# Moving a group's small work from before the scores to behind them, in a fused attention and soft mixture-of-experts kernel

## The chip, the cores and the metric

One Trainium2 chip, of which the kernel uses one core. The metric is device time in microseconds (us) of one execution, lower is better. TensorE is called PE here, its weight loads PEld, VectorE DVE, ScalarE ACT, GpSimd POOL and SyncE SP.

## The reference

```python
scale = 1.0 / S                                  # S = 2496, 8 batches, D = 256, d_qk = 64
attn = np.maximum(scale * (z @ z.T), 0.0) ** 2   # per batch
x = u * (attn @ v)                               # all tokens together: N = 19968
logits = x @ phi                                 # 32 slots: 8 experts of 4
d = softmax of logits over the tokens            # each slot's weights
slot_input = d.T @ x
slot_out = per expert: relu(slot_input @ w1) @ w2
c = softmax of logits over the slots             # each token's weights
out = c @ slot_out
```

The kernel computes all of it in one launch, with the transposed output.

## The kernel before

**Tiling.** The attention runs per batch over chunks of up to 512 queries (`chunks`, L150; a batch is 4 x 512 + 448, and the last one ends in two chunks of 256), and per chunk over 5 steps p of four key tiles of 128. A step has two half steps s = 0 and 1. `pair(i, w)` (L454) makes the scores of two key tiles of step i: six PE matmuls into the two tiles sc (L180 to L195), on ACT two relus and two squares (r, L199 and L203), on DVE the high part ph and the low part pl of each square (L205, L211). `attend` (L215) has the weighted sums of step i in its two half steps, 24 matmuls each into acc, from ph, pl and v; half step s first calls `between(s)`, which calls `pair(i + 1, s)`. So the scores run one step ahead of the sums that use them: the first half of a step needs the ph and pl that the half step before has made.

**The group's small work.** When 1024 tokens are done, `finish_chunk` (L275) starts a generator `groups(q)` (L292) and puts six calls of it into `work`; `between` takes one a half step, from p = 1 on. Call 1: the logits of the group into the PSUM tile lg (32 PE instructions in the trace), and into the same tile the slot sums of the group before it (`late`, `slot_sums`, L389; 32 more); on DVE the block that makes L, the running maximum and m (L316 to L324). Call 2 does nothing. Calls 3 and 4: sixteen transpositions each of the group's x into the tiles tr_0 and tr_1 (L335), and ACT's copy xt of each. Call 5: eight transpositions of L and E into the tile le and ACT's copy of it. There are 20 groups; 19 start inside the attention.

**What sets the order.** PE, ACT and DVE run in program order (`InOrder`, L39); each engine's queue is the order in which the code issues. Three lists hold closures for later: `begin` is emptied at the head of `between`, `middle` inside `scores` between the relus and the squares (L201), `behind` at the end of `scores` (L213). Into `middle` goes `exps` (the exponential E on ACT, L326), into `behind` goes `add_up` (L400: three DVE instructions that add the slot sums to slot_acc, reading the tile lg) and the splits of the next batch's z and v that have landed (`landing`). The tiles lg, tr, le and sl share the tag "ms" of `ms_ps` (L61), which has one buffer of two banks: a new one starts when the last reader of the one before is done.

Of the kernel before, what the change touches and what calls it, by code (L numbers as in the profile page):

```python
# [50 lines left out]
def attn_soft_moe_kernel(ctx, tc, uT, v, zz, phi, ww, outT):  # L51
# [19 lines left out]
    def load_z(b, j):  # L71
        raw = raws.tile([P, 512], F32, tag="zraw" if b == 0 else "raw", name=f"zr_{b}_{j}", bufs=NQ if b == 0 else NRAW)
        nc.sync.dma_start(raw, zz[b, :, j * 512 : (j + 1) * 512])
        zraw[b, j] = raw

        def split():
            t = zt[b, j] = blk.tile([P, 2, 512], F32R, tag="blk", name=f"z_{b}_{j}")
            for h in (1, 0):
                rows = HALF[h]
                act.copy(t[rows, h], raw[rows])  # L80
                dve.tensor_sub(t[rows, 1 - h], raw[rows], f32(t[rows, h]))

        return split

    def load_v(b, i):
        raw = raws.tile([P, 2, D], F32, tag="raw", name=f"vr_{b}_{i}", bufs=NRAW)
        nc.sync.dma_start(raw, v[b, :, 2 * i : 2 * i + 2, :])

        def split():
            t = vt_[b, i] = blk.tile([P, 2, 2, D], F32R, tag="blk", name=f"v_{b}_{i}")  # L90
            act.copy(t[:, :, 0], raw)
            dve.tensor_sub(t[:, :, 1], raw, f32(t[:, :, 0]))

        return split
# [8 lines left out]
    def open_loads(m):  # L103

        while opening and (len(v_splits) < m or opening[0][0] is load_z):
            f, j = opening.pop(0)
            (z_splits if f is load_z else v_splits).append(f(0, j))
# [61 lines left out]
    def run(todo):  # L169
        now, todo[:] = todo[:], []  # L170
        for f in now:
            f()

    def scores(b, ch, p, w):


        j, o, n, t0 = ch
        k0 = 4 * p + 2 * w
        ps = [sc_ps.tile([P, QC], F32, tag="sc", name=f"sc_{t0}_{k0 + h}") for h in range(2)]
        if t0 == 0:  # L180
            for h, rows in enumerate(HALF):
                c = 2 * w + h
                pe.matmul(
                    ps[h], zraw[b, p][rows, c * P : (c + 1) * P], zraw[b, 0][rows],
                    start=True, stop=True,
                )
        else:
            zk, zq = zt[b, p], zt[b, j]
            for m, (kl, ql) in enumerate(((0, 0), (0, 1), (1, 0))):
                for h, rows in enumerate(HALF):  # L190
                    c = 2 * w + h
                    pe.matmul(
                        ps[h][:, :n], zk[rows, h ^ kl, c * P : (c + 1) * P],
                        zq[rows, h ^ ql, o : o + n], start=(m == 0), stop=(m == 2),
                    )  # L195
        rs = []
        for h in range(2):
            r = wa.tile([P, QC], F32, tag="r", name=f"r_{t0}_{k0 + h}", bufs=5)
            act.activation(r[:, :n], ps[h][:, :n], AF.Relu, scale=1.0 / S)  # L199
            rs.append(r)  # L200
        run(middle)  # L201
        for kt, r in enumerate(rs, k0):
            act.activation(r[:, :n], r[:, :n], AF.Square)  # L203
            hi = wa.tile([P, QC], F32R, tag="ph", name=f"ph_{t0}_{kt}", bufs=7)
            dve.tensor_copy(hi[:, :n], r[:, :n])  # L205
            if t0 == N - 256 and kt == KT - 1:
                lo, rows = hi, HALF[1]
            else:
                lo = wa.tile([P, QC], F32R, tag="pl", name=f"pl_{t0}_{kt}", bufs=7)
                rows = HALF[1] if kt == KT - 1 else slice(0, P)  # L210
            dve.tensor_sub(lo[rows, :n], r[rows, :n], f32(hi[rows, :n]))  # L211
            pend[t0, kt] = hi, lo
        run(behind)  # L213

    def attend(b, ch, p, acc, between):  # L215


        j, o, n, t0 = ch
        todo = [[[], []], [[], []]]
        for kt in range(4 * p, 4 * p + 4):  # L220
            hi, lo = pend.pop((t0, kt))
            vt = vt_[b, kt // 2][:, kt % 2]
            hh, lh, hl = (vt[:, 0], hi), (vt[:, 1], hi), (vt[:, 0], lo)
            if kt < KT - 1:
                for s in range(2):
                    for h in range(2):
                        todo[s][h] += [hh, lh, hl]
            else:

                todo[0][0] += [hh, lh]  # L230
                todo[0][1] += [lh, hl]
                todo[1][0] += [hh]
                todo[1][1] += [hl]
        for s in range(2):
            between(s)
            before = turns[-1:]
            for i in range(len(todo[s][0])):
                for h, rows in enumerate(HALF):
                    vp, pp = todo[s][h][i]
                    c = h ^ s  # L240
                    x = pe.matmul(
                        acc[:, c, :n], vp[rows, c * P : (c + 1) * P], pp[rows, :n],
                        start=(p == 0 and s == 0 and i == 0),
                        stop=(p == NP - 1 and s == 1 and i == len(todo[s][h]) - 1),
                    )
                    while before:
                        await_(x, before.pop())
            turns.append(nc.gpsimd.nop())
            await_(turns[-1], x)
# [8 lines left out]
    def attend_whole(b, ch, p, acc):  # L258

        j, o, n, t0 = ch  # L260
        for kt in range(4 * p, 4 * p + 4):
            hi, lo = pend.pop((t0, kt))
            vt = vt_[b, kt // 2][:, kt % 2]
            prods = [(vt[:, 0], hi), (vt[:, 1], hi)] + ([] if lo is hi else [(vt[:, 0], lo)])
            for c in range(2):
                for i, (vp, pp) in enumerate(prods):
                    pe.matmul(
                        acc[:, c, :n], vp[:, c * P : (c + 1) * P], pp[:, :n],
                        start=False, stop=(kt == KT - 1 and i == len(prods) - 1),
                    )  # L270
# [161 lines left out]
    def load_w(pool, tag):  # L432
        i = len(w_raw)
        if i < NW:
            t = pool.tile([P, 2, 512], F32, tag=tag, name=f"w_{i}")
            nc.sync.dma_start(t, ww[i].rearrange("p (k n) -> p k n", k=2))
            w_raw.append(t)
# [4 lines left out]
    def load_u(b, ch):  # L442
        _, _, n, t0 = ch
        ut = wa.tile([P, 2, QC], F32, tag="ut", name=f"ut_{t0}", bufs=1)
        q0 = t0 - b * S
        nc.sync.dma_start(
            ut[:, :, :n], uT[b, :, q0 : q0 + n].rearrange("(c p) q -> p c q", p=P)
        )
        ut_[t0] = ut
# [4 lines left out]
    def pair(i, w):  # L454

        if i >= len(steps):
            run(middle)
            run(behind)
            return
        b, ch, p = steps[i]  # L460
        j, t0, q = ch[0], ch[3], 2 * p + w
        if q == 2:
            load_u(b, ch)
        if len(landing) > 1:
            behind.append(landing.pop(0))
        if b < B - 1:
            if j == NQ - 3 and w:
                landing.append(load_z(b + 1, p))
            m = -1
            if j == NQ - 2 and w:  # L470
                m = p
            elif j == NQ - 1 and q in (2, 4, 5, 7, 8):
                m = NQ + (2, 4, 5, 7, 8).index(q)
            if m >= 0:
                landing.append(load_v(b + 1, m))
        elif t0 >= N - 512 - 256 and t0 < N - 256:
            if len(w_raw) < NBLK - 15:
                load_w(blk, "blk")
        elif t0 == N - 256 and q >= 2:
            load_w(blk, "blk")  # L480
        if i % (NQ * NP) == 0 and w == 0 and landing:
            behind.append(landing.pop(0))
        scores(b, ch, p, w)
        if i < NP:
            v_splits.pop(0)()
            open_loads(NRAW)
        if b == 0 and z_splits and q % 2 and t0 + q >= 5:
            z_splits.pop(0)()
# [6 lines left out]
    for i, (b, ch, p) in enumerate(steps):  # L495
        if p == 0:
            acc = acc_ps.tile([P, 2, QC], F32, tag="acc", name=f"acc_{ch[3]}")

        def between(s):
            run(begin)  # L500
            if work and 2 * p + s > 1:
                work.pop(0)()
            pair(i + 1, s)

        if i + 1 < len(steps):
            attend(b, ch, p, acc, between)
        else:
            attend_whole(b, ch, p, acc)
        if p == NP - 1:
            finish_chunk(b, ch, acc)  # L510
# [223 lines left out]
```

## Time and profile before

| | before |
|---|---|
| median of 3 runs | 1521.64 us (1521.44 to 1525.31) |
| the profiled execution | 1521.83 us |
| its span, first to last instruction | 1519.6 us |
| mean granted PE clock | 0.987 |
| ACT's wait for scores | 367.5 us in 308 waits |
| DVE's wait for ACT's squares | 263.6 us in 261 waits |

All times in the prediction's rows come from the profiled execution and count from its first instruction; the time of the run is 2.2 us more than the span. A row of the timeline gives start, length, engine, line, operation, what is written and from what, the shapes, and in brackets the idle time in front and what ended it. Most of the lines read L47, since `InOrder` issues for all; so one goes by the tiles' names, in which buffer numbers are left out. "x6" merges six like instructions.

### The profile page before, as it was taken

The page shows a single profiled execution, that of the slowest core. Times are in us where ns is not written, and L with a number is a line of the kernel's source. Part 1 is how long each engine was busy: PE and PEld are TensorE (multiplying, and loading weights), DVE is VectorE, ACT ScalarE, POOL GpSimd, SP SyncE. Part 2 cuts the span into 40 slices and gives each one's busy share as a digit, 9 for nine tenths or more (in the row PEclk, how much of TensorE's full clock was granted, in tenths as well). Part 3 has the DMA queues.
Part 4 walks back from the last instruction along what each step waited for, and adds up shares of the span by engine and source line. Part 5 has one row for each costly group of instructions (what it writes and reads, how often), then busy time and mean ns, then how long its engine had stood idle before and what let it go on. Part 6 is the DMA issues. An engine that isn't in the chain of part 4 may idle for free.

```text
span 1519.6 us, 36942 instructions
## 1 busy us (share of the span) xinstructions
PE 1484.9 (98%) x14724; PEld 1226.0 (81%) x14724; DVE 1112.4 (73%) x2205; ACT 1025.7 (67%) x1987; POOL 3.2 (0%) x21
## 2 busy tenths in 40 slices
PE   8999999999999999999999999999999999999985
PEld 7987988788787888779777888789878798888853
DVE  6778776877678776787778776787767787676753
ACT  7777756867677766777567766677667776665543
POOL 0000000000000000000000000000000000000000
PEclk9999999999999999999999999999999999999995
DMA  4111100121001210111101120011101131000759
GB/s 133 29 36 49 56 23 27 42 56 50 16 22 50 55 36 15 36 50 55 26 19 56 42 57 16 22 50 55 36 15 36 50 118 54 16 15 9 264 226 392
DMA packets 36652, 91.53 MB, mean 60 GB/s; under 512 B 3712, under 2 KB 6272, under 8 KB 34432
## 3 DMA queue, kind: packets, MB, share of 16 engines
q1 hardware_dynamic: 36480, 89.18, 18.3%
q8 instruction: 116, 1.90, 0.5%
q14 instruction: 56, 0.46, 0.1%
HBM read 68.71 MB, written 20.45 MB: 59 GB/s over the span
## 4 chain that ended last, share of the span: by engine, by line
PE 91%; DVE 4%; DMA 2%; issue 1%; ACT 1%; DVEq 0%; SPq 0%; ACTq 0%
PE acc L47 67%; PE sc L47 18%; PE lg L47 2%; DMA outT<-ot 2%; PE tr L47 1%; DVE ph L47 1%; DVE pl L47 1%; DVE z L47 1%; PE h L582 0%; PE po L604 0%; DVE ot L664 0%; PE le L47 0%; PE pf L658 0%; ACT r L47 0%; DVE slot_acc L47 0%
## 5 line engine op out<-in xcount | busy, mean ns | idle before, releaser
L47 PE MATMUL acc<-ph,v 64*128 64x512 f32 (+2 forms) x6384 | 1009.8, 384 | 0.1
L47 PEld LDWEIGHTS acc<-ph,v 64*128 64x128 f32 x6384 | 638.9, 185 | 109.2 <-DVE ph L47 3.8
L47 ACT ACTIVATE r<-sc 128x512 f32<-128x512 f32 (+2 forms) x820 | 428.5, 575 | 369.8 <-PE sc L47 367.5
L47 PE MATMUL acc<-pl,v 64*128 64x512 f32 (+2 forms) x3190 | 666.2, 384 | 1.4
L47 DVE TENSOR_TENSOR pl<-r,ph 128x512 fp32r<-128x512 f32 (+4 forms) x819 | 546.0, 667 | 74.2 <-DVE ph L47 0.9
L47 DVE CAST ph<-r 128x512 fp32r<-128x512 f32 (+2 forms) x820 | 335.7, 409 | 266.6 <-ACT r L47 263.6
L47 ACT ACTIVATE r<-r 128x512 f32<-128x512 f32 (+2 forms) x820 | 455.2, 611 | 0.0
L47 PEld LDWEIGHTS acc<-pl,v 64*128 64x128 f32 x3190 | 336.4, 184 | 63.0 <-DVE pl L47 11.2
L47 PE MATMUL sc<-z,z 64*128 64x512 f32 (+2 forms) x1920 | 276.4, 385 | 0.0
L47 PEld LDWEIGHTS sc<-z,z 64*128 64x128 f32 x1920 | 181.8, 185 | 35.8 <-issue 6.6
L47 PE MATMUL sc<-z 64*128 64x512 f32 (+2 forms) x480 | 69.4, 386 | 0.0
L47 ACT COPY xt<-tr 128x1024 f32<-128x1024 f32 x39 | 39.6, 1015 | 28.8 <-PE tr L47 28.8
L47 DVE TENSOR_TENSOR z<-zr,z 64x512 fp32r<-64x512 f32 x80 | 55.0, 687 | 2.5
L47 DVE TENSOR_TENSOR v<-vr,v 128x512 fp32r<-128x512 f32 x80 | 54.9, 686 | 1.1 <-ACT v L47 0.8
L47 ACT CAST v<-vr 128x512 fp32r<-128x512 f32 x80 | 49.4, 618 | 8.9 <-PE sc L47 8.9
L47 PEld LDWEIGHTS sc<-z 64*128 64x128 f32 x480 | 45.6, 185 | 7.7 <-issue 1.6
L47 ACT CAST z<-zr 64x512 fp32r<-64x512 f32 x80 | 49.6, 620 | 2.0
L47 DVE TENSOR_TENSOR xg<-acc,ut 128x1024 f32<-128x1024 f32 (+7 forms) x56 | 48.8, 893 | 1.8 <-PE acc L47 1.8
L664 DVE COPY ot<-pf 128x1024 f32<-128x1024 f32 (+2 forms) x22 | 24.2, 1101 | 21.3 <-DMA outT<-ot 15.5
L658 PE MATMUL pf<-cp,soh 32*128 32x512 f32 (+2 forms) x176 | 24.5, 539 | 13.6 <-ACT ot L664 9.1
L664 ACT COPY ot<-pf 128x1024 f32<-128x1024 f32 (+2 forms) x22 | 20.2, 917 | 25.2 <-DMA outT<-ot 18.3
L658 PEld LDWEIGHTS pf<-cp,soh 32*128 32x128 f32 x176 | 12.9, 239 | 24.6 <-ACT ot L664 17.0
(92 smaller groups left out, 400.2 us busy)
## 6 DMA issues: line engine op xcount, KB each, us to landing
vr<-in_v SPq DMA_DIRECT2D x80, 256.0 KB, 2.7
w<-in_w SPq DMA_DIRECT2D x32, 512.0 KB, 6.6
outT<-ot SPq DMA_DIRECT2D x16, 1024.0 KB, 8.4
ut<-in_uT SPq DMA_DIRECT2D x31, 512.0 KB, 3.7
zr<-in_zz SPq DMA_DIRECT2D x40, 256.0 KB, 2.7
ut<-in_uT SPq DMA_DIRECT2D x8, 448.0 KB, 3.5
outT<-ot SPq DMA_DIRECT2D x4, 512.0 KB, 5.1
outT<-ot SPq DMA_DIRECT2D x2, 768.0 KB, 5.6
```

The costliest lines, as they stand in the source:

```text
L47: return lambda *a, **k: self.tc.keep_in_program_order(f(*a, **k))
L658: nc.tensor.matmul(pf[t // 2][:, t % 2, :ng], a[rows, c], parts[g0][rows, k, :ng], start=(m == 0), stop=(m == 2), tile_position=(t * NS, 0),)
L664: x = (nc.vector.tensor_copy if tp else nc.scalar.copy)(o, pf[tp][:, :, :ng])
```

## The change

In `between`, the group's piece of work is taken after `pair` instead of before it:

```diff
         def between(s):
             run(begin)
+            pair(i + 1, s)
             if work and 2 * p + s > 1:
                 work.pop(0)()
-            pair(i + 1, s)
```

No instruction is added or taken away. On PE, here for group 4 (the names hold the chunk's first token, 5504, the key tile 12 or 13, and the group), before:

```order
L47 MATMUL acc_5504_5916<-pl_5504_7_5986,v_2_3_4776 128x512 x2
L47 MATMUL tr_4_0_6154<-ident_76,xg_4_4846 128x64 x16
L47 MATMUL sc_5504_12_6172<-z_2_1_4040,z_2_3_4279 128x512
L47 MATMUL sc_5504_13_6173<-z_2_1_4040,z_2_3_4279 128x512
...
L47 MATMUL acc_5504_5916<-ph_5504_8_6070,v_2_4_4922 128x512 x4
```

and now:

```order
L47 MATMUL acc_5504_5916<-pl_5504_7_5986,v_2_3_4776 128x512 x2
L47 MATMUL sc_5504_12_6154<-z_2_1_4022,z_2_3_4279 128x512
L47 MATMUL sc_5504_13_6155<-z_2_1_4022,z_2_3_4279 128x512
...
L47 MATMUL tr_4_0_6176<-ident_76,xg_4_4846 128x64 x16
L47 MATMUL acc_5504_5916<-ph_5504_8_6026,v_2_4_4922 128x512 x4
```

The transpositions of call 3 have gone from in front of the six scores to between them and the sums; lg, tr_1 and le do the same in their half steps.

On DVE, from the last instruction of the block that makes m (call 1) to the first ph behind slot_acc, before:

```order
L47 TENSOR_SCALAR m_4_6048<-runmax0_84 128x1
L47 CAST ph_5504_8_6070<-r_5504_8_6063 128x512
L47 TENSOR_TENSOR pl_5504_8_6072<-r_5504_8_6063,ph_5504_8_6070 128x512
L47 CAST ph_5504_9_6075<-r_5504_9_6065 128x512
L47 TENSOR_TENSOR pl_5504_9_6077<-r_5504_9_6065,ph_5504_9_6075 128x512
L47 SCALAR_TENSOR_TENSOR slot_acc1_83<-slot_acc0_82,m_3_4985,lg_4_6013 128x256
L47 SCALAR_TENSOR_TENSOR slot_acc1_83<-slot_acc0_82,m_3_4985 128x1
L47 TENSOR_TENSOR slot_acc1_83<-slot_acc1_83,lg_4_6013 128x256
L47 CAST ph_5504_10_6120<-r_5504_10_6115 128x512
```

and now:

```order
L47 TENSOR_SCALAR m_4_6070<-runmax0_84 128x1
L47 CAST ph_5504_10_6117<-r_5504_10_6110 128x512
L47 TENSOR_TENSOR pl_5504_10_6119<-r_5504_10_6110,ph_5504_10_6117 128x512
L47 CAST ph_5504_11_6122<-r_5504_11_6112 128x512
L47 TENSOR_TENSOR pl_5504_11_6124<-r_5504_11_6112,ph_5504_11_6122 128x512
L47 SCALAR_TENSOR_TENSOR slot_acc1_83<-slot_acc0_82,m_3_5009,lg_4_6035 128x256
L47 SCALAR_TENSOR_TENSOR slot_acc1_83<-slot_acc0_82,m_3_5009 128x1
L47 TENSOR_TENSOR slot_acc1_83<-slot_acc1_83,lg_4_6035 128x256
L47 CAST ph_5504_12_6167<-r_5504_12_6162 128x512
```

The block and slot_acc both stand one pair later: behind the pair of tiles 8 and 9, and behind that of 10 and 11.

On ACT, around the exponential E, before:

```order
L47 ACTIVATE r_5504_8_6063<-sc_5504_8_6055 128x512
L47 ACTIVATE r_5504_9_6065<-sc_5504_9_6056 128x512
L47 ACTIVATE E_4_6047,m_4_6048<-L_4_6046,m_4_6048 128x256
L47 ACTIVATE m_4_6048<-m_4_6048 128x1
L47 ACTIVATE r_5504_8_6063<-r_5504_8_6063 128x512
L47 ACTIVATE r_5504_9_6065<-r_5504_9_6065 128x512
```

and now:

```order
L47 ACTIVATE r_5504_10_6110<-sc_5504_10_6102 128x512
L47 ACTIVATE r_5504_11_6112<-sc_5504_11_6103 128x512
L47 ACTIVATE E_4_6069,m_4_6070<-L_4_6068,m_4_6070 128x256
L47 ACTIVATE m_4_6070<-m_4_6070 128x1
L47 ACTIVATE r_5504_10_6110<-r_5504_10_6110 128x512
L47 ACTIVATE r_5504_11_6112<-r_5504_11_6112 128x512
```

E too stands one pair later, between that pair's relus and squares. The copies xt and le, which stood in front of the relus of their half step, now stand behind its squares and splits.

## The prediction

> **What bounds the kernel now.** I read the page first, then the chain that ended last, the list of waits, and the timeline around one group's small work.
>
> ```profile
> span 1519.6 us, 36942 instructions
> PE 1484.9 (98%) x14724; PEld 1226.0 (81%) x14724; DVE 1112.4 (73%) x2205; ACT 1025.7 (67%) x1987; POOL 3.2 (0%) x21
> PE 91%; DVE 4%; DMA 2%; issue 1%; ACT 1%; DVEq 0%; SPq 0%; ACTq 0%
> ```
>
> TensorE (PE) is busy for 98% of the span and is 91% of the chain. So whatever holds PE in the attention part is added to the time almost one for one, and an engine with slack counts only where PE waits for it. The plain rhythm, from the chain (start, length, what):
>
> ```profile
> 230.24 0.69 PE sc L47 x6
> 230.94 2.81 PE acc L47 x24
> 233.74 0.69 PE sc L47 x6
> ```
>
> A half step is 0.69 us of scores and 2.81 us of weighted sums, so scores start every 3.50 us. PE's waits inside this part, from the list of waits (total us, times, longest), are few:
>
> ```profile
> PEld acc L47 <- DVE pl L47: 11.2, 25, 0.5
> PEld acc L47 <- DVE ph L47: 3.8, 19, 0.3
> PE tr L47 <- DVE slot_acc L47: 1.6, 1, 1.6
> ```
>
> The first two, 15.0 us together, are all that earlier scores could win. The third matters most: once in the run a transposition waited for the running sum slot_acc.
>
> **The change part by part.** Nothing is added or removed. The group's piece of work moves behind `pair`, on PE behind the six scores. Three things move that the diff doesn't say. First, `groups` appends `exps` to `middle` and `add_up` to `behind`; both lists are emptied inside `pair`. Today `pair` comes right after, in the same half step; after the change these closures wait for the next half step's `pair`. Second, VectorE's (DVE) block that makes L and m stands behind this half step's ph and pl. Third, ScalarE's (ACT) copies of tr and le stand behind the squares and splits.
>
> `add_up` reads the logits' PSUM tile, and tag "ms" has one buffer. So tr_0, two half steps after lg, can't start before `add_up` has ended. I call the half step with lg H0, the next H1, the one with tr_0 H2. The replay uses the group whose tile before is named lg_4, all times before the change. PE first:
>
> ```profile
> 403.36 0.85 PE L47 MATMUL sc<-z 64*128 64x512 f32 x6
> 406.94 1.09 PE L47 MATMUL lg<-xg,phi_sb 64*32 64x256 f32 x32
> 412.43 0.86 PE L47 MATMUL sc<-z,z 64*128 64x512 f32 x6
> 415.95 0.66 PE L47 MATMUL tr<-ident,xg 64*128 64x64 f32 x16
> ```
>
> Then ACT and DVE in the same stretch:
>
> ```profile
> 404.24 1.09 ACT L47 ACTIVATE r<-sc 128x512 f32<-128x512 f32 x2 [1.36 <-PE sc L47]
> 405.21 1.16 ACT L47 ACTIVATE r<-r 128x512 f32<-128x512 f32 x2
> 410.83 0.51 ACT L47 ACTIVATE E<-L,m 128x256 f32<-128x256 f32 x1
> 411.43 1.14 ACT L47 ACTIVATE r<-r 128x512 f32<-128x512 f32 x2
> 413.32 1.09 ACT L47 ACTIVATE r<-sc 128x512 f32<-128x512 f32 x2 [0.75 <-PE sc L47]
> ```
>
> ```profile
> 407.47 0.69 DVE L47 TENSOR_TENSOR pl<-r,ph 128x512 fp32r<-128x512 f32 x1
> 409.00 0.42 DVE L47 COPY L<-lg 128x256 f32<-128x256 f32 x1 [0.84 <-PE lg L47]
> 410.64 0.15 DVE L47 TENSOR_SCALAR m<-runmax 128x1 f32<-128x1 f32 x1
> 413.61 0.69 DVE L47 TENSOR_TENSOR pl<-r,ph 128x512 fp32r<-128x512 f32 x1
> 414.22 0.47 DVE L47 SCALAR_TENSOR_TENSOR slot_acc<-slot_acc,m,lg 128x256 f32<-128x256 f32 x1
> 414.74 0.41 DVE L47 TENSOR_TENSOR slot_acc<-slot_acc,lg 128x256 f32<-128x256 f32 x1
> ```
>
> Today `add_up` ends at 414.74 + 0.41 = 415.15, and tr_0 at 415.95 passes freely: 0.80 us of slack. After the change, with the same durations:
>
> - H0's scores start at 403.36 + 3.50 = 406.86. The last pl of a pair ends 407.47 + 0.69 - 403.36 = 4.80 after its scores started: at 411.66. The logits are ready long before.
> - The L block takes 410.64 + 0.15 - 409.00 = 1.79, now behind that pl: until 413.45.
> - H1's scores start at 412.43 as today (lg has only changed places with the scores inside H0), its first relu at 413.32. The next ACT instruction starts 405.21 - 404.24 = 0.97 later, at 414.29, and that is now the exponential E; m has been ready since 413.45. E and its small companions take 411.43 - 410.83 = 0.60, so H1's squares start at 414.89.
> - From the first square to the end of the last pl: 413.61 + 0.69 - 411.43 = 2.87, so 417.76. `add_up` ends 415.15 - 414.30 = 0.85 after that: 418.61.
>
> What a transposition held by this sum takes to start again, from the 256-wide chunk near the end of the attention:
>
> ```profile
> 1399.81 0.42 DVE L47 TENSOR_TENSOR slot_acc<-slot_acc,lg 128x256 f32<-128x256 f32 x1
> 1400.37 0.71 PE L47 MATMUL tr<-ident,xg 64*128 64x64 f32 x16 [1.59 <-DVE slot_acc L47]
> ```
>
> 0.14 us after the sum's end (1400.23), so tr_0 starts at 418.75. By then PE has finished H2's scores at 415.95 + 0.69 = 416.64 and has nothing else in its order: the 24 sums of H2 stand behind tr_0, although their operands lie ready. PE is held for 418.75 - 416.64 = 2.11 us. Its queue is in order, so the whole rest shifts by that; behind it wait H3's scores, and ACT and DVE for those.
>
> How many groups pay (two rows of the groups by shape):
>
> ```profile
> L47 DVE SCALAR_TENSOR_TENSOR slot_acc<-slot_acc,m,lg 128x256 f32<-128x256 f32 x17 | 8.1, 475 | 0.0
> L47 DVE COPY slot_acc<-lg 128x256 f32<-128x256 f32 x1 | 0.4, 418 | 0.0
> ```
>
> Eighteen groups carry an `add_up` on the logits' tile. Seventeen lie in chunks 448 or 512 wide, the eighteenth is the 256-wide one that waits already. 17 x 2.11 = 35.9 us. A 448-wide pair is shorter on both engines alike, so I price it the same.
>
> Smaller terms. (a) In three of the seventeen, by ACT's order, H0's pair also splits a z half; its DVE part now stands ahead of the L block:
>
> ```profile
> L47 DVE TENSOR_TENSOR z<-zr,z 64x512 fp32r<-64x512 f32 x80 | 55.0, 687 | 2.5
> ```
>
> Two of 0.687 move the L block's end from 413.45 to 414.82, past 414.29; E then starts 0.5 to 0.6 later: 3 x 0.6 = +1.8. (b) The eighteenth group's wait of 1.59 grows by between 0 (the sum is late anyway) and 2.11; I take 0.7, nearer the end where a wait stands already. (c) tr_1 and le wait for the copies of tr, now behind the squares. That copy is about 1 us, and H2's hold gives ACT the time for it; only the first group, which has no `add_up`, can wait at tr_1. It has a z split of some 1.3 us ahead of the copy: between 0 and 1.3, I take +0.6. (d) le no longer delays the scores of its half step:
>
> ```profile
> 281.74 0.24 PE le L47 x8
> ```
>
> By ACT's order, eleven of the nineteen groups inside the attention have a split beside tr_0; there ACT and DVE carry the most, and their scores come 0.24 sooner: 11 x 0.24 = -2.6, with ends of 0 and -15.0 (all of those waits). (e) lg and tr now go from scores to sums instead of from sums to scores; both neighbours have one shape (64*128), so the switches cost the same: 0. SP's loads keep their order and half step, and POOL's list is the same: 0.
>
> Sum: 35.9 + 1.8 + 0.7 + 0.6 - 2.6 = +36.4 us. The profiled execution took 1521.83 for a span of 1519.6, and becomes 1558.2; on the median of the runs shown, 1521.64, it is **1558.0**, a ratio of 1.024.
>
> **The rivals.** *Earlier scores win.* If `add_up` still ends before PE wants tr_0, nothing is held, and scores that no longer stand behind lg take away the waits for ph and pl: with half of 15.0, 1514; with all, 1506.6. For it: ACT idles in front of the group's scores today and could start them about 2 us sooner. Against it: the two operations that decide are fixed by order, E behind H1's relus and `add_up` behind H1's last pl. The point from which it decides is 416.50, and the replay has 418.61; it would have to be 2.1 us wrong. Chance 0.02.
>
> *The buffer doesn't hold.* If tr_0's two banks were free without `add_up`, only terms (c) and (d) are left: 1521.64 + 0.6 - 2.6 = 1519.6, no change that could be told. The 1.59 us row above says that it does hold. 0.02.
>
> *The hold is shared.* If PE's hold lets DVE get ahead, so that the waits for ph and pl vanish afterwards, and the hold itself is 1.7 instead of 2.11 a group: 17 x 1.7 + 1.8 + 0.7 + 0.6 - 15.0 = +17.0, so 1538.6. DVE's order after H2 is paced by PE's scores, which come late together with everything; so I give it 0.08.
>
> *The clock falls.* The granted clock (the column after POOL) in two stretches:
>
> ```profile
> 1400.00:1409.00 9.00, 8.63 (x172) 8.00 (x174) 5.91 (x19) 6.05 (x16) 0.00 (x0) 1.00 0.01 2
> 1480.00:1485.00 5.00, 2.91 (x24) 1.65 (x22) 1.83 (x2) 1.01 (x1) 0.00 (x0) 0.65 1.00 418
> ```
>
> Right around the hold of 1.59 us it stayed 1.00; in the closing part, where PE is busy 2.91 of 5.00 us, it fell. If every hold of over 2 us made one half step of 3.50 us run at half the clock, 18 x 3.50 = 63 us come on top: 1621. The row at 1400 speaks against it, though at a shorter hold; 0.05. [...]
>
> **How the numbers follow.** The forecast has 0.83, the rivals 0.02, 0.02, 0.08 and 0.05. Range: the hold can be off by 0.4 us a group (17 x 0.4 = 6.8), the smaller terms' ends add some 3 upwards, and the waits of term (d) may go half (another 5) downwards: 1546 to 1568. About 0.3% (5 us) is what a measurement of this kernel can tell from no change. Faster by more than that: 0.02; within: 0.02; slower: 0.96.
>
> **What would show it.** In the profile after, the list of waits has tr waiting for slot_acc some 18 times with about 2.1 us each (2.7 in three), and PE's busy share falls to 95 or 96%. In the timeline E stands after H1's relus, slot_acc one half step later than today, with tr right behind it. The waits of sums for pl and ph are some us smaller. I am wrong if tr's wait is absent or under 1 us; if tr_1 or le wait for ACT's copies of tr by more than 3 us in all, term (c) was wrong; if the clock shows dips in the middle, the last rival was right.

## The result, and the profile after

The changed kernel takes 1575.05 us (median of six, 1572.72 to 1580.4), the kernel before beside it 1523.36 (1521.22 to 1525.31): a ratio of 1.035 (the quotient of the two medians is 1.034), 95% interval 1.0337 to 1.0363. Slower, as forecast, but by 51.7 us where the forecast said 36.4, and outside the range. The profiled execution took 1572.91 us. From the page of the changed kernel:

```profile
span 1570.8 us, 37017 instructions
PE 1498.7 (95%) x14724; PEld 1314.8 (84%) x14724; DVE 1111.1 (71%) x2205; ACT 1024.0 (65%) x1987; POOL 3.1 (0%) x21
PE 85%; DVE 6%; ACT 4%; issue 2%; DMA 2%; DVEq 0%; SPq 0%; ACTq 0%
```

PE has fallen from 98% to 95% of the span, and the chain now runs through DVE and ACT for 10% instead of 5%. But look at the busy time too: with the same 14724 instructions PE is busy for 1498.7 us instead of 1484.9. A wait alone can't do that; some matmuls have become longer (the 512-wide ones of acc from ph take 399 ns in the mean, in before 395). The list of waits (total us, times, longest):

```profile
PE tr L47 <- DVE slot_acc L47: 38.8, 18, 2.7
...
PEld acc L47 <- DVE pl L47: 10.2, 24, 0.5
...
PEld acc L47 <- DVE ph L47: 3.0, 14, 0.5
```

The third wait of the prediction has grown from one of 1.6 us to eighteen of 38.8 us in all. Here is the group of the replay, the one whose tile before is lg_4, from the timeline after:

```profile
420.69 0.69 DVE L47 TENSOR_TENSOR pl<-r,ph 128x512 fp32r<-128x512 f32 x1
...
421.30 0.42 DVE L47 COPY L<-lg 128x256 f32<-128x256 f32 x1
...
422.93 0.15 DVE L47 TENSOR_SCALAR m<-runmax 128x1 f32<-128x1 f32 x1
...
423.94 0.51 ACT L47 ACTIVATE E<-L,m 128x256 f32<-128x256 f32 x1
...
424.52 1.15 ACT L47 ACTIVATE r<-r 128x512 f32<-128x512 f32 x2
...
427.90 0.41 DVE L47 TENSOR_TENSOR slot_acc<-slot_acc,lg 128x256 f32<-128x256 f32 x1
...
428.47 0.71 PE L47 MATMUL tr<-ident,xg 64*128 64x64 f32 x16 [2.03 <-DVE slot_acc L47]
```

H0's scores start at 416.50 in this trace, where the replay had 406.86, so 9.64 has to be added to the replay's times. It then puts the L block's end at 423.09 (measured 422.93 + 0.15 = 423.08), E at 423.93 (423.94), the squares at 424.53 (424.52), the end of add_up at 428.25 (427.90 + 0.41 = 428.31) and tr_0 at 428.39 (428.47). The order of events and the hold (2.03 for 2.11) are as forecast.

So 38.8 - 1.6 = 37.2 us of the span's 51.2 (1570.8 - 1519.6) are holds. The other 14 us I put down to the clock, which the experiments then test. The mean over the span (0.987 before), then windows of the changed kernel (PE's busy time and, in the column after POOL, the granted clock):

```profile
core 0: 1570.8 us, clock 0.978
```

```profile
351.77:355.18 3.41, 1.33 (x26) 1.06 (x24) 3.20 (x9) 2.93 (x7) 0.00 (x0) 1.00 0.00 0
355.18:358.59 3.41, 3.41 (x22) 3.41 (x20) 1.98 (x4) 0.73 (x1) 0.00 (x0) 0.50 0.41 92
358.59:362.00 3.41, 3.41 (x48) 3.38 (x46) 0.90 (x2) 2.48 (x5) 0.00 (x0) 1.00 0.19 67
423.45:426.86 3.41, 2.99 (x26) 2.07 (x22) 1.54 (x4) 2.61 (x8) 0.00 (x0) 1.00 0.00 0
426.86:430.27 3.41, 1.80 (x28) 1.80 (x30) 3.20 (x8) 2.75 (x5) 0.00 (x0) 1.00 0.00 0
430.27:433.69 3.42, 3.42 (x44) 3.30 (x42) 0.32 (x1) 0.95 (x2) 0.00 (x0) 1.00 0.00 0
795.50:798.91 3.41, 1.53 (x25) 1.47 (x27) 3.10 (x9) 2.79 (x5) 0.00 (x0) 1.00 0.00 0
798.91:802.32 3.41, 3.41 (x19) 2.98 (x17) 0.59 (x1) 0.23 (x1) 0.00 (x0) 0.50 0.00 0
1017.37:1020.78 3.41, 1.57 (x14) 0.94 (x10) 2.36 (x5) 3.20 (x9) 0.00 (x0) 1.00 0.03 11
1020.78:1024.19 3.41, 2.62 (x34) 2.55 (x36) 3.17 (x8) 2.50 (x4) 0.00 (x0) 1.00 0.02 5
```

The second row is 3.41 us at half the clock: PE counts as busy throughout and gets 22 instructions done, where the next row has 48; the 448-wide matmuls of acc from ph take 543 ns in the mean there and 394 in the next row. The trace's record of the clock has nine such dips between the opening and the closing part (before had none), each 3.413 us long, starting at 280.09, 355.18, 573.63, 723.82, 798.91, 874.00, 945.68, 1095.87 and 1450.86. All these starts lie whole multiples of 3.413 us apart (355.18 - 280.09 = 75.09 = 22 x 3.413): in this trace the clock changes on one grid. The rows above are cut on that grid, and a window is one step of it. The holds with a dip behind them are 2.03 to 2.65 us long, those without 2.01 to 2.63: what tells them apart is how they fall into the grid. The hold of 2.08 us in the first row lies within that one window, PE is busy there for 1.33 us, and the next window runs at half clock. The hold of 2.03 at 428.47 is split over two windows with 2.99 and 1.80 busy, and nothing happens. In this trace a dip follows every window of the attention with 1.53 us busy or less (1.88 us idle or more), and none with 1.57 or more. Nine of eighteen holds fell on the wrong side.

### The profile page after: what moved, and what is told of

Its sections match the earlier page's. It is cut to its first block, busy times and chain, and to the rows that moved or that the text cites. A ratio compares the mean times of both kernels' runs of the same rounds, so it can differ in the third digit from the quotient of the medians.

```text
span 1570.8 us, 37017 instructions
## 1 busy us (share of the span) xinstructions
PE 1498.7 (95%) x14724; PEld 1314.8 (84%) x14724; DVE 1111.1 (71%) x2205; ACT 1024.0 (65%) x1987; POOL 3.1 (0%) x21
## 3 DMA queue, kind: packets, MB, share of 16 engines
q1 hardware_dynamic: 36480, 89.18, 17.7%
## 4 chain that ended last, share of the span: by engine, by line
PE 85%; DVE 6%; ACT 4%; issue 2%; DMA 2%; DVEq 0%; SPq 0%; ACTq 0%
PE acc L47 63%; PE sc L47 16%; ACT r L47 2%; DMA outT<-ot 2%; PE lg L47 2%; DVE ph L47 2%; PE tr L47 1%; DVE pl L47 1%; DVE slot_acc L47 1%; DVE z L47 1%; ACT E L47 1%; PE h L582 0%; PE po L604 0%; DVE ot L664 0%; DVE v L47 0%
## 5 line engine op out<-in xcount | busy, mean ns | idle before, releaser
L47 PE MATMUL acc<-ph,v 64*128 64x512 f32 (+2 forms) x6384 | 1049.8, 389 | 0.3 <-DVE ph L47 0.3
L47 PEld LDWEIGHTS acc<-ph,v 64*128 64x128 f32 x6384 | 683.6, 187 | 73.1 <-issue 7.6
L47 PE MATMUL acc<-pl,v 64*128 64x512 f32 (+2 forms) x3190 | 689.8, 387 | 1.1
L47 PEld LDWEIGHTS acc<-pl,v 64*128 64x128 f32 x3190 | 362.7, 187 | 40.2 <-DVE pl L47 9.4
L47 PEld LDWEIGHTS sc<-z,z 64*128 64x128 f32 x1920 | 199.5, 185 | 19.9
L47 PEld LDWEIGHTS tr<-ident,xg 64*128 64x128 f32 x624 | 25.8, 140 | 47.7 <-issue 45.8
L47 PE MATMUL tr<-ident,xg 64*128 64x64 f32 x624 | 27.7, 227 | 39.1 <-DVE slot_acc L47 38.8
L47 PEld LDWEIGHTS sc<-z 64*128 64x128 f32 x480 | 49.4, 184 | 4.5
L664 DVE COPY ot<-pf 128x1024 f32<-128x1024 f32 (+2 forms) x22 | 24.2, 1101 | 21.1 <-DMA outT<-ot 15.4
```

The lines of the kernel that those rows point to most:

```text
L47: return lambda *a, **k: self.tc.keep_in_program_order(f(*a, **k))
L664: x = (nc.vector.tensor_copy if tp else nc.scalar.copy)(o, pf[tp][:, :, :ng])
```

## The experiments

My theory after this: a hold costs its own length, and about half of the holds also one window at half the clock. Rivals: the 14 us come from the new position itself (switches of PE, operands that come later); or the loss is simply in proportion to the hold.

**Fill the pause.** PE gets 0.46 us more work ahead of tr_0, in products that are written over again (`fill` is true in the half step with tr_0; the entries of `work` hold a mark for it); the release should not move.

```diff
-            for m, (kl, ql) in enumerate(((0, 0), (0, 1), (1, 0))):
+            for m, (kl, ql) in [(3, (0, 0))] * (2 * fill[-1]) + list(enumerate(((0, 0), (0, 1), (1, 0)))):
...
-                        zq[rows, h ^ ql, o : o + n], start=(m == 0), stop=(m == 2),
+                        zq[rows, h ^ ql, o : o + n], start=(m in (0, 3)), stop=(m in (2, 3)),
...
+            fill.append(bool(work) and 2 * p + s > 1 and work[0][0])
             pair(i + 1, s)
```

> The changed kernel, and in the half step with tr_0 the first product of the scores is issued three times instead of once (four more score matmuls of some 0.115 us each, which only write the same values again), so that PE works 0.46 us longer before it is held at tr_0. add_up's end is set by the half step before and should not move. Theory (the hold costs its own length, and half of the holds also cost a window of 3.41 us at half the clock, because PE was idle for 1.88 us or more inside one window of a fixed grid): tr_0 starts where it did, PE's idle time falls from 2.03-2.08 to 1.57-1.62 us in fourteen groups and from 2.6 to 2.1 in three, so the dips go, but for at most three, and with them some 14 us: 1560 to 1565 us, tr's wait 30 to 31 us in all. Rival (the 14 us beside the holds come from the new position itself, such as more switches or later operands, not from the clock): 1575 to 1577 us with the same waits. The added matmuls by themselves make the kernel slower, so a shorter time can come from the clock alone.

Measured: 1564.59 us, ratio 1.0267 (1.0252 to 1.0282). That is some 10 us faster than the changed kernel, with more work. Its wait, and windows on its grid:

```profile
PE tr L47 <- DVE slot_acc L47: 31.1, 18, 2.2
```

```profile
274.86:278.28 3.42, 1.55 (x14) 0.94 (x10) 2.82 (x7) 2.79 (x6) 0.00 (x0) 1.00 0.00 0
278.28:281.69 3.41, 3.08 (x38) 2.99 (x40) 3.14 (x7) 2.43 (x4) 0.00 (x0) 1.00 0.00 0
349.96:353.37 3.41, 1.74 (x30) 1.40 (x28) 3.20 (x9) 2.92 (x6) 0.00 (x0) 1.00 0.02 5
353.37:356.78 3.41, 3.41 (x48) 3.30 (x46) 1.73 (x4) 1.31 (x3) 0.00 (x0) 1.00 0.43 100
1435.40:1438.81 3.41, 1.37 (x32) 1.19 (x30) 2.83 (x9) 1.85 (x6) 0.00 (x0) 1.00 0.02 5
1438.81:1442.22 3.41, 3.41 (x40) 3.41 (x38) 0.72 (x2) 1.06 (x2) 0.00 (x0) 0.50 0.01 2
```

The third row is the same group as the first row of the changed kernel: the whole hold lies in one window again, but with the filling PE is busy for 1.74 instead of 1.33, and the clock stays. Only the last hold, with 1.37 busy, is followed by half clock. The holds are still there and eight of the nine dips are gone, so the dips are a cost of their own, and the rival of the position falls. It is not luck of the grid either: fourteen of these holds are 1.58 to 1.67 us long, less than the 1.88 of idle time that stood before every dip of the changed kernel. The first row narrows the edge: 1.55 busy passes, 1.53 above did not.

**Take the hold away in three ways.** `add_up` at once, where the slot sums are issued:

```diff
-            behind.append(lambda: add_up(ps))
+            add_up(ps)
```

> The changed kernel, but add_up is issued at once where the slot sums are, so on VectorE it stands behind H0's pl and ahead of the L block instead of one half step later. Theory (hold plus clock): tr_0 waits for nothing, no dips in the middle, and what is left is the change without its hold: 1519 to 1524 us. Rival (the new position costs something by itself, the 14 us beside the holds): 1533 to 1538 us. Rival (earlier scores win once the hold is gone, the waits for ph and pl vanish): 1507 to 1514 us.

Measured: 1523.38 us, 1.0007 (0.9998 to 1.0017). Then only lg behind the pair, and only the others behind it (`work` holds a mark for call 1; the first of the two is shown, the other has True and False exchanged):

```diff
-            pair(i + 1, s)
-            if work and 2 * p + s > 1:
-                work.pop(0)()
+            first, call = work.pop(0) if work and 2 * p + s > 1 else (None, None)
+            if first is False:
+                call()
+            pair(i + 1, s)
+            if first is True:
+                call()
```

> Half of the change: only the call with lg stands behind the pair; the calls with tr_0, tr_1, le and the slot sums stand in front of the scores as before. Then tr_0 waits for the same add_up, but PE has not yet done H2's 0.69 us of scores. Theory: holds of 2.7 to 2.8 us (3.3 in the three groups with a z split) eighteen times, some +50 us, and dips behind about thirteen of them (idle of 1.88 us inside one window of 3.41 us becomes likelier with a longer hold), 1.6 us each, +21: 1585 to 1600 us. Without the clock's part: 1570 to 1575. Rival (the calls with tr and le in their new place are what costs): 1523 to 1530.

> The other half of the change: the call with lg stands in front of the scores as before, the calls with tr_0, tr_1, le and the slot sums behind them. add_up and the L block stay in their half step. Theory: no hold at tr_0, no dips, 1519 to 1524 us. Rival (the place of tr and le is what costs): 1535 us or more, with waits of tr_1 or le for ScalarE's copies of tr.

Measured: with lg alone behind, 1598.29 us, 1.0482 (1.046 to 1.0505); with lg alone in front, 1521.54 us, 0.999 (0.9981 to 0.9999). And one more empty call between lg and tr_0:

```diff
         middle.append(exps)
         yield
         yield
+        yield
...
-                work.extend([lambda it=it: next(it, None)] * 6)
+                work.extend([lambda it=it: next(it, None)] * 7)
```

> The changed kernel with add_up where the change put it, and one more empty call between lg and tr_0, so tr_0 comes one half step later. Theory: add_up ends about 0.7 us or more before PE wants tr_0, no hold, no dips: 1519 to 1524 us. If PE still waits at tr_0, the buffer is held by something other than add_up.

Measured: 1520.61 us, 0.9989 (0.998 to 0.9998). With add_up at once tr_0 never waits for it. With lg alone in front it waits once, in the 256-wide chunk, and with one more empty call once for 0.2 us; the two rows, in this order:

```profile
PE tr L47 <- DVE slot_acc L47: 0.9, 1, 0.9
```

```profile
PE tr L47 <- DVE slot_acc L47: 0.2, 1, 0.2
```

The three versions without the hold are all back at the time of before, so the new place of lg, tr and le costs nothing that counts, and the whole loss hangs on tr_0 waiting for add_up. The two halves of the change are not alike: lg behind the scores delays add_up and is all of the loss; with tr behind the scores too, PE does their 0.69 us of work before it is held, which is why lg alone is worse than the full change:

```profile
PE tr L47 <- DVE slot_acc L47: 50.7, 18, 3.3
```

The version with add_up at once shows the cover of the prediction's term (c) gone. Its waits have a row of PE's that the changed kernel has only once, for 0.4 us:

```profile
PE tr L47 <- ACT xt L47: 3.9, 7, 0.9
```

With no hold at tr_0, ACT has less time to catch up, and tr_1 waits for its copy of tr.

**Shorter and longer holds.** `add_up` between the two key tiles of H1's pair (a list `half`, emptied behind each pl), and one pair later:

```diff
-            behind.append(lambda: add_up(ps))
+            half.append(lambda: add_up(ps))
...
             pend[t0, kt] = hi, lo
+            run(half)
```

> The changed kernel, but add_up is issued on VectorE between the two key tiles of H1's pair instead of behind both, so it ends about one ph and pl (some 1.0 us) earlier. Theory (a hold costs its length, and a window of half clock comes only where PE is idle for about 1.88 us or more inside one window of 3.41 us): holds of 1.0 to 1.1 us, 1.6 to 1.7 in the three groups with a z split, some 18 us in all, and no dip in the middle at all: 1538 to 1543 us, that is about half of the holds but only a third of the loss. Rival (the loss is in proportion to the hold, 51.7 us for 37.2 us of holds): 1545 to 1549 us.

```diff
-            behind.append(lambda: add_up(ps))
+            behind.append(lambda: behind.append(lambda: add_up(ps)))
```

> The changed kernel, but add_up stands one more pair later on VectorE, behind H2's pl. Theory: tr_0 is held until H2's whole chain is through, 5.0 to 5.2 us eighteen times, 90 to 94 us; and since such a hold always leaves 1.88 us or more of one window idle, a dip follows each of the eighteen, at 1.6 us or more, now and then two windows long: 1640 to 1670 us. Rival (loss in proportion to the hold): 1646 to 1652, with dips behind only part of the holds. Rival (only the holds cost): 1611 to 1616.

Measured: 1540.15 us, 1.0121 (1.0106 to 1.0137), and 1644.48 us, 1.0807 (1.0792 to 1.0822). The shorter holds are 0.9 to 1.0 us, and 1.5 in the three groups with a z split, a little under the theory's. Their rows, the wait and the mean clock, which is that of before:

```profile
PE tr L47 <- DVE slot_acc L47: 19.3, 18, 1.6
```

```profile
core 0: 1537.8 us, clock 0.988
```

And of the longer, with windows on its grid around one hold of 5.02 us:

```profile
PE tr L47 <- DVE slot_acc L47: 87.7, 18, 5.0
```

```profile
438.28:441.69 3.41, 0.00 (x0) 0.00 (x0) 2.55 (x5) 1.83 (x4) 0.00 (x0) 1.00 0.00 0
441.69:445.10 3.41, 2.12 (x22) 2.02 (x24) 1.14 (x4) 0.97 (x1) 0.00 (x0) 0.50 0.00 0
445.10:448.52 3.42, 3.42 (x18) 2.89 (x18) 0.00 (x0) 0.05 (x1) 0.00 (x0) 0.50 0.00 0
448.52:451.93 3.41, 3.41 (x42) 2.85 (x42) 0.46 (x2) 2.20 (x5) 0.00 (x0) 1.00 0.00 0
```

One window is idle from end to end, and the next two run at half clock. A dip follows each of the eighteen holds, as the theory had it, but fifteen of them last two windows, not only now and then, and the holds are a little shorter than its 5.0 to 5.2 us (4.7 to 5.0, and 3.8 in the eighteenth). The time of 1644.48 alone hardly tells the theory from the rival of proportion (1646 to 1652); the clock's record and the shorter hold do. The accounts of the profiled executions, against before (span 1519.6, wait 1.6), in us; the windows are counted in the trace's clock record between the opening and the closing part:

| kernel | span longer by | tr's wait longer by | left | windows at half clock |
|---|---|---|---|---|
| add_up half a pair earlier | 18.2 | 17.7 | 0.5 | 0 |
| the change, pause filled | 39.7 | 29.5, and 8.7 of filling (19 x 0.46) | 1.5 | 1 |
| the change | 51.2 | 37.2 | 14.0 | 9 |
| lg alone behind | 69.7 | 49.1 | 20.6 | 12 |
| add_up a pair later | 123.8 | 86.1 | 37.7 | 33 |

The left part follows the windows, not the hold: 1.6 us a window in the change, 1.7 with lg alone, 1.1 where the hold itself takes up part of the slow window. Of the filled kernel's 1.5, and of the 37.7 in the last row, 1.2 and 1.6 us lie behind the last weighted sum: the closing part took 87.9 and 88.3 us in these two, 86.6 in before. Half of the hold's length (17.7 of 37.2) brought none at all, so the rival of proportion falls: it asked for 1545 to 1549.

**Where PE's other waits come from.** The trace of before has a wait on ACT that no term of mine used, the exponential of the combine weights, in the middle of a pair:

```profile
ACT cw L47 <- DVE cw L47: 15.4, 18, 1.7
```

```profile
284.92 1.26 ACT L47 CAST z<-zr 64x512 fp32r<-64x512 f32 x2
286.27 1.09 ACT L47 ACTIVATE r<-sc 128x512 f32<-128x512 f32 x2
289.04 0.42 ACT L47 ACTIVATE cw<-cw 128x256 f32<-128x256 f32 x1 [1.68 <-DVE cw L47]
289.36 1.14 ACT L47 ACTIVATE r<-r 128x512 f32<-128x512 f32 x2
```

The relus are done, the squares are ready to go, and ACT stands still for 1.68 us for cw. In the kernel before, with nothing else changed:

```diff
-            middle.append(combine_exp)
+            behind.append(combine_exp)
```

> The kernel before, with one closure put into another list: the exponential of the combine weights cw is appended to behind instead of middle, so on ScalarE it stands behind the next pair's squares and no longer waits there for VectorE. In the kernel before ScalarE waits 18 times for cw, 15.4 us in all. Theory (PE's few waits of the middle part come from ScalarE being late after that): up to 10 us fewer, 1511 to 1518 us. Rival (ScalarE has slack there and PE never sees it): 1520 to 1523 us, with the row of cw gone.

Measured: 1513.49 us, 0.9948 (0.9935 to 0.996). The same stretch and the waits:

```profile
284.48 1.09 ACT L47 ACTIVATE r<-sc 128x512 f32<-128x512 f32 x2
285.45 1.15 ACT L47 ACTIVATE r<-r 128x512 f32<-128x512 f32 x2
287.24 0.42 ACT L47 ACTIVATE cw<-cw 128x256 f32<-128x256 f32 x1 [0.63 <-DVE cw L47]
```

```profile
PEld acc L47 <- DVE pl L47: 3.0, 9, 0.5
...
ACT cw L47 <- DVE cw L47: 2.5, 4, 0.6
```

The squares go at once, and of the 15.0 us that sums waited for pl and ph, 3.0 are left; the time is 8.2 us shorter. Then this together with each of the three ways without a hold: lg in front of the scores and the rest behind; one more empty call; add_up at once.

> Both findings together: the call with lg in front of the scores and the others behind them (no hold), and the exponential of cw put into behind (the run before it won 8.2 us from the kernel before). Theory (the two act in different half steps, so they add): 1521.5 - 8.2 = 1513, between 1511 and 1515 us. Rival (tr and le behind the scores also lose their waits once ScalarE is on time): 1505 to 1510 us. Rival (E or the squares now come late behind the moved exponential): 1516 or more.

> The change's order with one more empty call between lg and tr_0 (no hold), and the exponential of cw put into behind. Theory (they add): 1520.6 - 8.2 = 1512.4, between 1510 and 1515 us. Rival (scores that stand behind no lg, tr or le lose all their waits once ScalarE is on time, some 10 us of sums waiting for pl): 1503 to 1508 us.

> The change with add_up issued at once (no hold), and the exponential of cw put into behind. Theory (they add): 1523.4 - 8.2 = 1515, between 1512 and 1517 us. Rival (the waits for pl vanish as well): 1505 to 1510 us.

Measured: 1511.27 us, 0.9932 (0.9919 to 0.9946); 1514.6, 0.9947 (0.9935 to 0.996); 1515.0, 0.9952 (0.994 to 0.9965). All three lie in the ranges of their theories. The first has the shortest time of all, 11.7 us below the kernel before beside it; its waits of PE for pl and for slot_acc are down to

```profile
PE tr L47 <- DVE slot_acc L47: 0.9, 1, 0.9
...
PEld acc L47 <- DVE pl L47: 0.7, 4, 0.2
```

Its interval and that of the moved exponential alone (0.9935 to 0.996) overlap, so what the new place of tr and le adds is not told apart by the times. In the traces, one of each, the last weighted sum ends 1.85 us earlier with it (at 1422.51 against 1424.36).

## Why the prediction was right about the hold and wrong about the time

- **The hold.** Right. Forecast 2.11 in the plain groups, measured 2.03 to 2.08 in thirteen and 2.01 in the first; forecast 2.7 in the three groups with a z split, measured 2.59 to 2.65; forecast 1.59 + 0.7 in the eighteenth, measured 2.29. That 0.7 was picked from between 0 and 2.11, so its fit is luck. In all 35.9 + 1.8 + 0.7 = 38.4 against 37.2.
- **tr_1 and le, term (c).** +0.6 forecast, 0.4 measured in one wait, and the version with add_up at once shows that the hold does hide the rest (3.9 us on PE without it).
- **le no longer in front of the scores, term (d).** The waits for pl and ph went from 15.0 to 10.2 + 3.0 = 13.2: -1.8 against -2.6. That le did this is not shown: ACT's wait for cw, which the moved exponential shows to be behind most of these waits, fell as well, from 15.4 us to

```profile
ACT cw L47 <- DVE cw L47: 10.8, 13, 1.4
```

  The versions with lg alone in front and with one more empty call, at 0.999 and 0.9989, are some 1.5 us faster than before and no more.
- **Earlier scores.** Of these 15.0 us of waits 12.0 could be taken away, and 8.2 us of the time with them, as the moved exponential shows, but by another cause than this rival named: not lg in front of the scores but cw in front of the squares.
- **The clock: the step that failed.** These measured terms give 37.2 + 0.4 - 1.8 = 35.8, as good as the forecast's 36.4. The missing 51.2 - 35.8 = 15.4 falls on nine windows of 3.413 us at half the clock, 1.71 each, which is half of such a window. The sum has nothing for it. The prediction had this only as a rival of 0.05, which struck at all eighteen holds or at none and cost 3.50 each; its wording, that dips in the middle would make it right, fits, but its 1621 does not: the price is half and the condition another. What spoke against it, "the row at 1400", was a hold of 1.59 us, while before each dip of the changed kernel PE was idle for 1.88 us or more of one window. So it was no evidence about 2.11. And the range was built as if the clock would fall behind every hold or behind none, and reached to 1568 for the sizes of the holds and small terms alone.

Holds of 2.03 us were enough: behind those that ended at 573.10 and 945.10 in the changed kernel the clock fell at 573.63 and 945.68. The grid's place against the kernel's first instruction differs between traces: the first dip, at 280.09 in the changed kernel and at 1438.81 with the filling, comes about 0.2 and 1.8 us after a whole number of windows. The trace of before had a warning that I did not read. Windows around the fall of the clock in its closing part, and PE's row in the list of waits from 1474 to 1482:

```profile
1474.67:1478.09 3.42, 1.90 (x28) 0.98 (x24) 3.42 (x5) 2.96 (x4) 0.00 (x0) 1.00 1.02 431
1478.09:1481.50 3.41, 2.05 (x26) 1.16 (x22) 2.51 (x3) 1.02 (x2) 0.00 (x0) 1.00 1.03 428
1481.50:1484.91 3.41, 2.01 (x14) 1.16 (x12) 1.23 (x1) 1.00 (x1) 0.00 (x0) 0.50 1.02 428
```

```profile
PE pf L658 <- DVE ot L664: 3.6, 5, 0.8
```

The clock fell there, at 1481.53, behind a window with 2.05 us busy, with no wait of PE over 0.8 us: no single long gap stands before this fall. Behind the window before it, with only 1.90 busy, the clock stayed, so the edge of the attention does not hold there. For the attention, that edge and the length of the grid give an estimate of the cost. A hold of 2.03 us puts 1.88 us or more into one window in (3.41 - 2.03 + 2 x 0.15) / 3.41 = 0.49 of its positions, one of 2.63 in 0.67; 15 x 0.49 + 3 x 0.67 = 9.4 dips at 1.7 us = 16 us, and 36.4 + 16 = 52.4 on the median, where 51.7 was measured. The edge was read from this same kernel, so the fit proves little; the test is in the kernels forecast with it before they ran: at most three dips with the filling, about thirteen with lg alone, none with the shorter hold and eighteen with the longer, where the traces have 1, 11, 0 and 18. It may account for the spread too: three runs of the changed kernel lie at 1572.7 to 1572.9 with a mean clock of 0.978, three at 1577.2 to 1580.4 with 0.972 to 0.974. That the second three had more dips in the attention, for another position in the grid, is argued from their clock and not shown. Part of the spread has another source: the kernel before, which has no such holds, splits as well, into 1521.2 to 1521.6 and 1525.1 to 1525.3.

## What to carry to other kernels

Price a new pause of the bounding engine twice: its length, and what it does to the clock afterwards; here a pause that left PE busy for 1.53 us or less of a clock window of 3.41 cost about another half window, and for pauses of 2 to 3 us it is a matter of position which do. When work is moved in program order, follow the closures it carries and the buffer that its last reader holds: here one line delayed the reader by a half step, and a shorter path for that one reader (add_up at once, or one empty step more) gave everything back. And read the waits of the engines that have slack: ACT's 15.4 us for cw, on an engine busy for 67%, was where most of PE's remaining waits began.

## What was not expected of the hardware

- In the trace of the changed kernel the granted clock changes on a grid of 3.413 us: nine dips of that length, whole multiples of it apart. In the attention of that kernel and in the rows above of the filled one, from full clock, half clock follows a window with PE busy for 1.53 us or less and not one with 1.55 or more (of 3.41).
- That edge is not general. In the closing part of the kernel before, whose matmuls of pf have the shape 32*128 there, the clock fell behind a window with 2.05 busy and not behind the one before it with 1.90, so PE's busy time in the last window alone does not tell these two apart; and in the attention, once the clock was low, it stayed so behind a window with 2.12 busy (the row at 441.69). What exactly brings a fall stays open.
- Filling a pause with useless products made the kernel about 10 us faster (1564.59 against 1575.05), though tr_0 was released no earlier (31.1 us of waits and 18 x 0.46 = 8.3 of filling, against 38.8 of waits).
